# A two-layer feed-forward stage by seven products: when the next pair's first weights and its input are prepared

## The chip, the cores and the metric

The kernel runs on one core of one Trainium2 chip. The metric is the device time of one execution in microseconds (us); the median of three executions stands for a kernel. A "span" is the time from the first to the last instruction that the profiler recorded. PE is the matmul engine (PEld its weight loads), DVE the vector engine, ACT the scalar engine, POOL is GpSimd and SP the engine whose queue issues all DMAs here.

## The reference

Three things are computed one after the other: windowed attention, a gated feed-forward layer, and the layer that matters here, which takes its input `x` of 2304 tokens by 512:

```python
def _moe2_ref(x, w_in, w_out) -> np.ndarray:      # x 2304 x 512, w_in 512 x 2048, w_out 2048 x 512
    h = x @ w_in
    sp = np.where(h > 20.0, h, np.log1p(np.exp(np.minimum(h, 20.0))))
    g = h * np.tanh(sp)
    return (g @ w_out).astype(np.float32)
```

## The kernel before

The last layer is `layer2` (L739), some 380 us at the end of the span. It works on three **pairs** of token groups (`NPB` = 3, each of 2 x 384 tokens). Both of its products are done by a 2 x 2 scheme with seven products in place of eight (`ORDER1` and `ORDER2`, L742 and L743), whose operands are sums and differences of quarters of the matrices. Every float32 operand is split in two parts, a rounded one and the rest: `hi_act` (L123) writes the first on ACT, `lo_dve` (L126) the second on DVE, and `part` (L661) issues both. Three matmuls of 128 x 128 by 384 columns (`products`, L706) make one float32 product of the parts.

For each pair there are two stages, called the hidden and the out stage below.

**Hidden stage.** Eight blocks (`NJ` = 8, `hidden`, L769), each seven products of two chunks, so 42 matmuls a block and 336 a stage. Block j needs the weight tile `win[p, j]` with the seven combinations in two parts. `make_win` (L753) builds it: four subtractions on POOL into the single buffer `t4` (L758), then two `hi_act` and two `lo_dve` (the lines L124 and L127 of the profile). Its input is loaded by `load_raw` (L749, a DMA of 512 KB on SP into one of two buffers `w4`). In the loop (L827) block j first issues `make_win` for block j + 2 and `load_raw` for block j + 4, as long as these lie in the same pair. The sums that leave a block are added on DVE (`add`, L665 and its line L666) and go through an activation on ACT (`mish`, L1001) into the tiles `G`.

**Out stage.** The loop over `ORDER2` = 4, 1, 6, 7, 2, 5, 3 (L844): seven products, each over four operand tiles `op` (`operands`, L797), 28 tiles in all, 12 matmuls each. An operand tile is one `part` of a quarter of `G` (one ACT and one DVE instruction), and around it stand sums of quarters on DVE (L803 to L811). There are five `op` buffers, so tile n can be written only after PE has done with tile n - 5. The weights `wout` come by DMA, 1 MB for every two operand tiles, into three buffers. When a product is complete, `outputs` (L715) adds its bank on DVE into the tiles `u` (shown as `v` in this stage) and `y`.

**What is prepared for the next pair.** After the last block, `load_x` (L678) loads the next input into `xr` with two DMAs of 768 KB, and the first two `load_raw` of the next pair are issued (L835 to L838). After product 7 the seven input operands `xs` are made by `x_parts` (L690): seven `part` and four sums of quarters (`sums4`, L668), so 7 instructions on ACT and 11 on DVE. After products 2 and 5 the first two weight tiles of the next pair are built (L887 to L890). `xr` and the `win` tiles share the tag `win`, of which the pool `br` (L983) has three buffers; a buffer is taken up again when its last reader is done.

**What sets the order.** PE's order is the order of the program (`manual_schedule`, L892). The queues of ACT, DVE, POOL and SP are put in order when the program is built (`schedule_with_timeline_sim`, L1052): by a modelled timeline, within what the data and the buffers allow, so that work may stand on its queue long before the place where the program names it. On the chip each queue then runs in that fixed order. `tc.issue_after(ins)` puts what is traced under it, on the engine of `ins`, behind `ins` on that engine's queue; it adds no wait for `ins` to finish.

Of the kernel before, what the change touches and what calls it, by code (L numbers as in the profile page):

```python
# [9 lines left out]
F32 = mybir.dt.float32  # L10
# [4 lines left out]
AF = mybir.ActivationFunctionType  # L15
ALU = mybir.AluOpType
# [11 lines left out]
NPB = NT // (2 * TB)  # L28
NJ = NF2 // 2
# [67 lines left out]
def body(ctx: ExitStack, tc: tile.TileContext, qT, kT, vP, w1, w1o, w2, cst, yT):  # L97
    nc = tc.nc
# [22 lines left out]


    def hi_act(out, in_):  # L123
        nc.scalar.activation(out=out, in_=in_, func=AF.Copy)  # L124

    def lo_dve(out, in_, hi):  # L126
        nc.vector.tensor_tensor(out=out, in0=in_, in1=hi.bitcast(F32), op=ALU.subtract)  # L127

    plansA = []
    t = 0  # L130
# [523 lines left out]
    def bank():  # L654
# [3 lines left out]
            return rot("bk")  # L658
        return ps.tile([128, 512], F32, tag=f"acc{c % CT}", name="bk", bufs=1)

    def part(x, src):  # L661
        hi_act(x[:, 0], src)
        lo_dve(x[:, 1], src, x[:, 0])

    def add(out, a, b, op=ALU.add):  # L665
        nc.vector.tensor_tensor(out=out, in0=a, in1=b, op=op)  # L666
# [20 lines left out]
    def x_tiles(bp, which):  # L687
        return {i: bp.tile([128, 2, 2, TB], F32R, tag=f"xs{i}", name=f"xs{i}", bufs=1) for i in which}
# [50 lines left out]
    def layer2(br):  # L739
        G = {}  # L740
        win, wout = {}, {}
        ORDER1 = (1, 6, 7, 5, 2, 4, 3)  # L742
        ORDER2 = (4, 1, 6, 7, 2, 5, 3)  # L743
        onto = {2: 1, 3: 5}
        onto2 = {2: 1}

        raws = {}

        def load_raw(p, j):  # L749
            raws[p, j] = br.tile([128, 4, 256], F32, tag="w4", name="w4", bufs=2)  # L750
            nc.sync.dma_start(out=raws[p, j], in_=w2d[j].rearrange("p (k n) -> p k n", k=4))

        def make_win(p, j):  # L753

            w = raws.pop((p, j))
            x = t4
            for o, a, b in ((0, w[:, 0], w[:, 1]), (1, w[:, 3], x[:, 0]), (2, w[:, 3], w[:, 0]), (3, x[:, 1], w[:, 2])):
                nc.gpsimd.tensor_tensor(out=x[:, o], in0=a, in1=b, op=ALU.subtract)  # L758
            t = win[p, j] = br.tile([128, 2, 7, 256], F32R, tag="win", name="win")
            for d, src in ((slice(0, 3), w[:, 1:4]), (slice(3, 7), x)):  # L760
                hi_act(t[:, 0, d], src)
                lo_dve(t[:, 1, d], src, t[:, 0, d])

        def load_wout(p, i, k):
            t = bp.tile([128, NJ // 2, 2, 256], F32R, tag="wout", name="wout", bufs=3)
            wout[p, i, k] = t
            nc.sync.dma_start(out=t.bitcast(F32), in_=w2o[SLOT[i], :, k * (NJ // 2):(k + 1) * (NJ // 2)])

        def hidden(p, j, xs):  # L769
            w = win.pop((p, j))  # L770
            q, jj = divmod(j, 2)
            if jj == 0:
                G[p, q] = bp.tile([128, 4, 2, TB], F32, tag=f"g{q}", name="G", bufs=1)
            g = G[p, q]
            u = {}

            def new():
                return bp.tile([128, TB], F32, tag="u", name="u", bufs=6)

            def done(k, a, b):  # L780
                if b is None:
                    mish(g[:, k, jj], a)
                    return
                add(g[:, k, jj], a, b, ALU.subtract if k == 2 else ALU.add)
                mish(g[:, k, jj], g[:, k, jj])

            bks = {}
            for i in ORDER1:
                bk = bks[i] = bks[onto[i]] if i in onto else bank()
                s = SLOT[i]  # L790
                products(
                    bk, [(w[:, 0, s, c:c + 128], w[:, 1, s, c:c + 128]) for c in (0, 128)],
                    [(xs[i][:, 0, c], xs[i][:, 1, c]) for c in range(2)], i not in onto, i not in onto.values(),
                )
                outputs(i, bk, u, new, done, True)

        def operands(p, i):  # L797

            for q in range(NJ // 2):
                g = G[p, q]  # L800
                o = bp.tile([128, 2, 2, TB], F32R, tag="op", name="op", bufs=5)
                if i == 6:
                    add(g[:, 0], g[:, 3], g[:, 0], ALU.subtract)  # L803
                part(o, g[:, {4: 3, 1: 0, 6: 0, 7: 2, 2: 1, 5: 3, 3: 2}[i]])
                yield o
                if i == 4:
                    add(g[:, 3], g[:, 2], g[:, 3])
                if i == 1:
                    add(g[:, 2], g[:, 0], g[:, 2], ALU.subtract)
                if i == 7:  # L810
                    add(g[:, 2], g[:, 1], g[:, 0], ALU.subtract)  # L811

        load_raw(0, 0)
        t4 = br.tile([128, 4, 256], F32, tag="t4", name="t4", bufs=1)
        xs = x_tiles(br, (7, 5))
        xr = load_x(br, 0)
        xs.update(x_tiles(br, (1, 4, 6, 2, 3)))
        load_raw(0, 1)
        x_parts(xs, xr)
        for j in range(2):  # L820
            make_win(0, j)
            load_raw(0, j + 2)
        bp, mish = yield
        yr = yT.rearrange("(c p) t -> p c t", p=128)
        for p in range(NPB):
            loads = [(i, k) for i in ORDER2 for k in range(2)]
            for j in range(NJ):  # L827
                if j + 2 < NJ:
                    make_win(p, j + 2)
                if j + 4 < NJ:  # L830
                    load_raw(p, j + 4)
                if j >= NJ - 3:
                    load_wout(p, *loads.pop(0))
                hidden(p, j, xs)
            if p + 1 < NPB:  # L835
                xr = load_x(br, p + 1)
                for j in range(2):
                    load_raw(p + 1, j)  # L838
            us = [{}, {}]
            ys = [[bp.tile([128, 2, TB], F32, tag="y", name="y", bufs=4) for _ in range(2)] for _ in range(2)]  # L840
            held = {}
            left = [[2, 2], [2, 2]]
            t0 = 2 * p * TB
            for i in ORDER2:  # L844
                bks = held[i] = held[onto2[i]] if i in onto2 else [bank(), bank()]
                for q, o in enumerate(operands(p, i)):
                    k, jq = divmod(2 * q, NJ // 2)
                    if (p, i, k) not in wout:
                        load_wout(p, i, k)
                        loads.remove((i, k))  # L850
                    w = wout[p, i, k]
                    if jq == 0 and loads:
                        load_wout(p, *loads.pop(0))
                    for m in range(2):
                        products(
                            bks[m],
                            [(w[:, jq + e, 0, 128 * m:128 * m + 128], w[:, jq + e, 1, 128 * m:128 * m + 128]) for e in range(2)],
                            [(o[:, 0, e], o[:, 1, e]) for e in range(2)],
                            i not in onto2 and q == 0, i not in onto2.values() and q == NJ // 2 - 1,
                        )  # L860
                for m in range(2):

                    def done(k, a, b, m=m):
                        t, f = divmod(k, 2)
                        y = ys[f][m]
                        if b is None:
                            nc.scalar.activation(out=y[:, t], in_=a, func=AF.Copy)
                        else:
                            add(y[:, t], a, b, ALU.subtract if k == 2 else ALU.add)
                        left[f][m] -= 1  # L870
                        if not left[f][m]:
                            nc.sync.dma_start(out=yr[:, 2 * f + m, t0:t0 + 2 * TB], in_=y.rearrange("p a t -> p (a t)"))

                    def new():
                        return bp.tile([128, TB], F32, tag="u", name="v", bufs=6)

                    if i == 4:
                        us[m]["p4"] = bks[m][:, :TB]
                        continue
                    outputs(i, bks[m], us[m], new, done, False)  # L880
                    if i == 7:
                        done(2, us[m]["b"], us[m]["p4"])
                if p + 1 < NPB:
                    if i == 7:
                        xs = x_tiles(br, range(1, 8))
                        x_parts(xs, xr)
                    if i in (2, 5):  # L887
                        j = (2, 5).index(i)
                        make_win(p + 1, j)
                        load_raw(p + 1, j + 2)  # L890

    with tc.manual_schedule(engines={mybir.EngineType.PE}):  # L892
        nc.sync.dma_start(out=cst_sb, in_=cst)
# [25 lines left out]
        while at < lasts[0]:  # L919
# [11 lines left out]
            f = (at / lasts[0] - CFG["conv_a"]) / (CFG["conv_b"] - CFG["conv_a"])  # L931
# [124 lines left out]
```

## Time and profile before

| | us |
|---|---|
| median of three executions | 1024.19 |
| lowest and highest of the three | 1022.73 and 1025.08 |
| the profiled execution | 1022.81 |
| its span | 1021.0 |
| layer 2 in it, first to last matmul | 637.0 to 1017.2 |

The profiled execution took 1.8 us more than its span: that lies around the recorded instructions. In the timeline view a row is a start, a length, an engine, a source line and an operation with its output and input; several like instructions in a row are merged ("x3"), and a bracket gives the idle time of the engine ahead of it and what ended that. In the view by windows each engine has its busy time and its instructions in the stretch, then come the granted clock of PE as a share of full speed, the DMA share and GB/s. The mean length of an instruction on DVE or ACT holds some overlap with the next one: of two in a row the starts are what counts.

### The profile page before, as it was taken

To read this page: it belongs to the slowest core of one execution; us is meant where nothing else is said; L and a number is where in the kernel's file an instruction comes from. 1 tells how busy PE (TensorE), PEld (TensorE's weight loads), DVE (VectorE), ACT (ScalarE), POOL (GpSimd) and SP (SyncE) were. 2 spreads that over 40 slices of the span, in tenths; PEclk is the share of its full clock that TensorE was granted. 3 is DMA by queue.
4 is the path that set the end of the run, shared out by engine and by line. 5 is a ranking of instruction groups with operands and counts; after the bars stand their busy time and mean duration, and the time that the engine had idled before them with its cause. 6 is when DMAs were issued, how large, how long until landed. Compare 5 with 4: busy or idle time off the path is not lost.

```text
span 1021.0 us, 14513 instructions
## 1 busy us (share of the span) xinstructions
PE 982.3 (96%) x5168; PEld 861.5 (84%) x5168; DVE 704.1 (69%) x1247; ACT 550.5 (54%) x1121; POOL 183.2 (18%) x204
## 2 busy tenths in 40 slices
PE   7899999999999999999999999599999999999998
PEld 5566777899987777787888999599899998999998
DVE  5988887777667644558643666877974888757773
ACT  6867565767666654545543345456453564335442
POOL 3700000000000000000002342542821429113000
PEclk9989999999999999999999999799999999999999
DMA  8844423476354622336401997513685236850275
GB/s 314 287 193 134 158 80 115 146 245 204 84 186 142 225 84 61 110 111 235 159 22 63 329 367 257 210 63 104 226 288 187 83 121 231 292 160 21 69 258 189
DMA packets 74936, 173.90 MB, mean 170 GB/s; under 512 B 8432, under 2 KB 50032, under 8 KB 65136
## 3 DMA queue, kind: packets, MB, share of 16 engines
q1 hardware_dynamic: 74864, 172.98, 51.0%
q8 instruction: 40, 0.66, 0.2%
q14 instruction: 32, 0.26, 0.1%
HBM read 137.30 MB, written 35.65 MB: 169 GB/s over the span
## 4 chain that ended last, share of the span: by engine, by line
PE 77%; DVE 8%; DMA 5%; POOL 5%; ACT 2%; issue 2%; SPq 1%; DVEq 0%; ACTq 0%; POOLq 0%
PE g_ps L117 28%; PE bk L117 24%; PE acc L117 14%; PE o_ps L117 5%; POOL t L758 4%; PE s_ps L117 4%; PE t_ps L259 3%; DMA wout<-w2o 2%; DVE G L666 1%; DVE win L127 1%; DMA wraw<-w 1%; DVE op L127 1%; POOL Pt L249 1%; DVE xs L127 1%; DVE xr L666 1%
## 5 line engine op out<-in xcount | busy, mean ns | idle before, releaser
L117 PE MATMUL g_ps<-xt,w 128*128 128x512 f32 (+1 forms) x1440 | 322.2, 375 | 0.3 <-ACT PT L271 0.3
L117 PEld LDWEIGHTS g_ps<-xt,w 128*128 128x128 f32 x1440 | 259.5, 188 | 40.3 <-issue 3.3
L117 PE MATMUL bk<-xs,win 128*128 128x384 f32 x1008 | 179.4, 337 | 14.2 <-ACT xs L124 8.0
L117 PEld LDWEIGHTS bk<-xs,win 128*128 128x128 f32 x1008 | 176.4, 189 | 16.9 <-ACT xs L124 8.3
L117 PE MATMUL bk<-op,wout 128*128 128x384 f32 x1008 | 180.9, 340 | 6.4 <-DVE op L127 4.9
L117 PEld LDWEIGHTS bk<-op,wout 128*128 128x128 f32 x1008 | 177.6, 191 | 9.2 <-DVE op L127 6.7
L117 PE MATMUL acc<-hh,ring 128*128 128x512 f32 (+1 forms) x480 | 149.7, 374 | 0.0
L758 POOL TENSOR_TENSOR t<-w 128x256 f32<-128x256 f32 x48 | 82.3, 1735 | 195.6 <-DVE win L127 184.5
L117 PEld LDWEIGHTS acc<-hh,ring 128*128 128x128 f32 x480 | 89.0, 188 | 13.8 <-issue 1.9
L124 ACT ACTIVATE op<-G 128x768 fp32r<-128x768 f32 x84 | 69.1, 841 | 47.3 <-PE bk L117 44.1
L127 DVE TENSOR_TENSOR op<-G,op 128x768 fp32r<-128x768 f32 x84 | 79.5, 957 | 21.7 <-ACT op L124 21.6
L117 PE MATMUL acc<-hl,ring 128*128 128x512 f32 (+1 forms) x240 | 88.4, 368 | 0.0
L230 ACT ACTIVATE Pt<-Pt,sm 128x256 f32<-128x256 f32 (+2 forms) x160 | 74.6, 467 | 16.7 <-DVE sm L226 16.3
L226 DVE CUSTOM_DVE_ANT_0 Pt<-s_ps,cst_sb 128x256 f32<-128x256 f32 (+2 forms) x160 | 54.3, 376 | 34.9 <-PE s_ps L117 34.8
L602 ACT ACTIVATE t<-g_ps 128x512 f32<-128x512 f32 (+1 forms) x60 | 33.1, 551 | 78.3 <-PE g_ps L117 78.3
L603 DVE SCALAR_TENSOR_TENSOR t<-t,g_ps 128x512 f32<-128x512 f32 (+1 forms) x60 | 37.7, 628 | 52.5 <-ACT t L602 52.4
L611 DVE SCALAR_TENSOR_TENSOR t<-t,g_ps 128x512 f32<-128x512 f32 (+1 forms) x60 | 37.9, 632 | 43.6 <-PE g_ps L117 42.7
L209 POOL MEMSET sm<- 128x8 f32 x40 | 5.3, 144 | 338.4 <-ACT Pt L247 310.2
L541 POOL TENSOR_TENSOR cw<-cw 128x256 f32<-128x256 f32 x32 | 30.4, 971 | 192.7 <-DMA cw<-w2d 192.2
L666 DVE TENSOR_TENSOR G<-u,bk 128x384 f32<-128x384 f32 x72 | 39.3, 553 | 36.0 <-PE bk L117 33.8
L1001 ACT ACTIVATE G<-G 128x384 f32<-128x384 f32 x72 | 37.0, 519 | 49.3 <-DVE G L666 49.3
L124 ACT ACTIVATE hh<-t 128x512 fp32r<-128x512 f32 (+1 forms) x60 | 34.9, 582 | 52.6 <-DVE t L611 52.6
(71 smaller groups left out, 1313.3 us busy)
## 6 DMA issues: line engine op xcount, KB each, us to landing
wout<-w2o SPq DMA_DIRECT2D x42, 1024.0 KB, 5.4
wraw<-w SPq DMA_DIRECT2D x16, 1024.0 KB, 5.4
w2o<-chl SPq DMA_DIRECT2D x16, 896.0 KB, 5.9
wst<-w SPq DMA_DIRECT2D x12, 1024.0 KB, 8.0
cw<-w1od SPq DMA_DIRECT2D x24, 512.0 KB, 4.0
w<-w2d SPq DMA_DIRECT2D x24, 512.0 KB, 3.4
w2d<-cw SPq DMA_DIRECT2D x16, 512.0 KB, 3.6
wraw<-w1o SPq DMA_DIRECT2D x6, 1024.0 KB, 6.0
```

Of the source, the lines that this page charges most:

```text
L117: nc.tensor.matmul(out=out, lhsT=lhsT, rhs=rhs, start=start, stop=stop, skip_group_check=True)
L124: nc.scalar.activation(out=out, in_=in_, func=AF.Copy)
L127: nc.vector.tensor_tensor(out=out, in0=in_, in1=hi.bitcast(F32), op=ALU.subtract)
L226: nc.vector.tensor_tensor_reduce(out=Pt[:q.qn, :w], in0=s_ps[:q.qn, q.so:q.so + w], in1=nb[:q.qn, 128 - q.kn:128 + q.qn], op0=ALU.add, op1 ...
L230: nc.scalar.activation(out=Pt[:q.qn, :w], in_=Pt[:q.qn, :w], func=AF.Exp, scale=-1.0, bias=sm[:q.qn, i:i + 1], accum_out=sm[:q.qn, 8 + i:9 ...
L259: nc.tensor.transpose(t_ps[:x.n, o:o + q.qn], Pt[:q.qn, c0:c0 + x.n], ident[:q.qn, :q.qn])
L602: tanhs.append(nc.scalar.activation(out=t[:, :n], in_=st["g"][:, :n], func=AF.Tanh, scale=0.5))
L603: nc.vector.scalar_tensor_tensor(out=t[:, :n], in0=t[:, :n], scalar=1.0, in1=st["g"][:, :n], op0=ALU.add, op1=ALU.mult)
L611: nc.vector.scalar_tensor_tensor(out=t[:, :n], in0=t[:, :n], scalar=0.5, in1=vps[:, :n], op0=ALU.mult, op1=ALU.mult)
L666: nc.vector.tensor_tensor(out=out, in0=a, in1=b, op=op)
L758: nc.gpsimd.tensor_tensor(out=x[:, o], in0=a, in1=b, op=ALU.subtract)
L1001: nc.scalar.activation(out=out, in_=in_, func=AF.Mish)
```

## The change

`make_win` and `load_raw` run on over the end of a pair: the blocks j = 6 and 7 build the first two weight tiles of the next pair, the blocks 4 to 7 load the raw weights of its first four. The calls after the last block and after products 2 and 5 go. `part` keeps the two instructions that it issued last, and `x_parts` is called under `tc.issue_after` for both: its ACT instructions stand behind the last ACT instruction of product 7's operands, its DVE instructions behind the last such DVE instruction.

```diff
     def hi_act(out, in_):
-        nc.scalar.activation(out=out, in_=in_, func=AF.Copy)
+        return nc.scalar.activation(out=out, in_=in_, func=AF.Copy)
 
     def lo_dve(out, in_, hi):
-        nc.vector.tensor_tensor(out=out, in0=in_, in1=hi.bitcast(F32), op=ALU.subtract)
+        return nc.vector.tensor_tensor(out=out, in0=in_, in1=hi.bitcast(F32), op=ALU.subtract)
...
+    latest = []
+
     def part(x, src):
-        hi_act(x[:, 0], src)
-        lo_dve(x[:, 1], src, x[:, 0])
+        latest[:] = hi_act(x[:, 0], src), lo_dve(x[:, 1], src, x[:, 0])
...
             for j in range(NJ):
-                if j + 2 < NJ:
-                    make_win(p, j + 2)
-                if j + 4 < NJ:
-                    load_raw(p, j + 4)
+                for f, k in ((make_win, p * NJ + j + 2), (load_raw, p * NJ + j + 4)):
+                    if k < NPB * NJ:
+                        f(*divmod(k, NJ))
                 if j >= NJ - 3:
                     load_wout(p, *loads.pop(0))
                 hidden(p, j, xs)
             if p + 1 < NPB:
                 xr = load_x(br, p + 1)
-                for j in range(2):
-                    load_raw(p + 1, j)
...
-                if p + 1 < NPB:
-                    if i == 7:
-                        xs = x_tiles(br, range(1, 8))
+                if p + 1 < NPB and i == 7:
+                    xs = x_tiles(br, range(1, 8))
+                    with tc.issue_after(latest[0].ins), tc.issue_after(latest[1].ins):
                         x_parts(xs, xr)
-                    if i in (2, 5):
-                        j = (2, 5).index(i)
-                        make_win(p + 1, j)
-                        load_raw(p + 1, j + 2)
+
```

## Rows read from the trace of the kernel before

**Rows 1.** The page, part 1: busy time, share of the span, instructions
```profile
PE 982.3 (96%) x5168; PEld 861.5 (84%) x5168; DVE 704.1 (69%) x1247; ACT 550.5 (54%) x1121; POOL 183.2 (18%) x204
```
**Rows 2.** Windows: the out stages of the three pairs, one after the other
```profile
711.02:774.28 63.26, 60.82 (x338) 59.69 (x337) 50.19 (x61) 29.50 (x40) 27.30 (x8) 0.97 0.71 243
...
833.85:898.35 64.50, 61.07 (x337) 59.63 (x337) 50.18 (x61) 29.50 (x40) 27.29 (x8) 0.97 0.70 238
...
957.94:1017.75 59.81, 58.71 (x337) 58.09 (x336) 38.11 (x48) 22.28 (x30) 0.00 (x0) 1.00 0.64 208
```
**Rows 3.** Timeline of PE, from the first pair's hidden stage to the end
```profile
672.95 14.86 PE L117 MATMUL bk<-xs,win 128*128 128x384 f32 x84 [0.52 <-DVE G L666]
688.02 23.16 PE L117 MATMUL bk<-xs,win 128*128 128x384 f32 x132 [0.21 <-DVE G L666]
...
732.37 14.47 PE L117 MATMUL bk<-op,wout 128*128 128x384 f32 x72 [1.99 <-DVE op L127]
747.30 27.14 PE L117 MATMUL bk<-op,wout 128*128 128x384 f32 x155 [0.46 <-DVE op L127]
...
855.20 14.45 PE L117 MATMUL bk<-op,wout 128*128 128x384 f32 x72 [1.98 <-DVE op L127]
...
889.95 8.56 PE L117 MATMUL bk<-op,wout 128*128 128x384 f32 x48 [0.98 <-DMA wout<-w2o]
...
957.94 50.11 PE L117 MATMUL bk<-op,wout 128*128 128x384 f32 x288
1008.57 8.59 PE L117 MATMUL bk<-op,wout 128*128 128x384 f32 x48 [0.51 <-DMA wout<-w2o]
```
**Rows 4.** Windows within the first pair's out stage, and within the third's
```profile
711.02:730.39 19.37, 19.37 (x110) 18.70 (x109) 19.37 (x23) 12.89 (x19) 11.03 (x1) 1.00 0.62 204
...
732.37:740.00 7.63, 7.63 (x35) 7.63 (x36) 6.03 (x7) 1.46 (x2) 7.63 (x3) 0.78 0.43 140
...
977.30:991.35 14.05, 14.05 (x83) 14.05 (x82) 11.08 (x14) 5.59 (x7) 0.00 (x0) 1.00 0.80 268
991.35:1017.75 26.40, 25.30 (x145) 24.68 (x143) 12.26 (x18) 7.66 (x10) 0.00 (x0) 1.00 0.59 197
```
**Rows 5.** Timeline of all engines around the start of the first out stage
```profile
703.93 0.85 ACT L124 ACTIVATE win<-w 128x768 fp32r<-128x768 f32 x1
...
719.36 20.32 POOL L758 TENSOR_TENSOR t<-w 128x256 f32<-128x256 f32 x2 [8.63 <-DVE win L127]
...
720.07 0.95 DVE L127 TENSOR_TENSOR op<-G,op 128x768 fp32r<-128x768 f32 x1
...
721.81 0.95 DVE L127 TENSOR_TENSOR xs<-xr,xs 128x768 fp32r<-128x768 f32 x1
...
725.28 0.95 DVE L127 TENSOR_TENSOR xs<-xr,xs 128x768 fp32r<-128x768 f32 x1
726.15 0.95 DVE L666 TENSOR_TENSOR G<-G 128x768 f32<-128x768 f32 x1
...
727.35 0.84 ACT L124 ACTIVATE op<-G 128x768 fp32r<-128x768 f32 x1
...
741.23 1.06 ACT L124 ACTIVATE win<-t 128x1024 fp32r<-128x1024 f32 x1 [6.29 <-POOL t L758]
```
**Rows 6.** The weight tile's POOL line L758 by tile: lengths min/median/max in ns
```profile
L758 POOL TENSOR_TENSOR t<-t,w x24: 728/741/1338, 629.8 to 935.2; 128x256 f32<-128x256 f32 x24
```
**Rows 7.** Timeline of DVE in the third out stage, around product 7's last operand
```profile
981.93 0.96 DVE L127 TENSOR_TENSOR op<-G,op 128x768 fp32r<-128x768 f32 x1
...
984.60 0.95 DVE L127 TENSOR_TENSOR op<-G,op 128x768 fp32r<-128x768 f32 x1
...
991.12 1.01 DVE L666 TENSOR_TENSOR v<-v,bk 128x384 f32<-128x384 f32 x2
```
**Rows 8.** Timeline of SP: the first pair's loads of the next input and of `wout`
```profile
696.65 1.20 SPq L682 DMA_DIRECT2D xr<-x2d  x2
...
715.39 0.33 SPq L767 DMA_DIRECT2D wout<-w2o  x1
```

## The prediction

> **What bounds the kernel.** The page's first part comes first: PE is busy for 96% of the span and DVE for 69% [rows 1], so a gain must come from time that PE loses, and only a stage in which DVE is short can lose it. The windows by stage show where that is. The three out stages do the same 336 matmuls, yet the first two take 63.26 and 64.50 us from their first matmul to the next stage's, and in both DVE is busy for 50.2 us; the third prepares no next pair, DVE has 38.1 us of work, and it takes 59.22 us (957.94 to 1008.57 + 8.59) [rows 2, 3]. The reader is to see that the two stages that prepare the next pair lose 4.04 and 5.28 us against the third, 9.32 us together. That is the whole stake at the pair boundaries.
>
> The timeline of PE says what the loss is made of. In the first pair PE waits 1.99 us for an operand's DVE part. In the next 7.63 us the granted clock is 0.78, so part of the time is at the lower of PE's two levels, 1.2 in place of 2.4 GHz, and the 72 matmuls take 14.47 us. At the third stage's rate (50.11 us for 288, 0.174 us each) they would take 12.53, so the clock costs 1.94 us more. A wait of 0.46 us follows [rows 3, 4]. The second pair repeats it, with 1.98 us, and adds a wait of 0.98 us for `wout`; the third has such a `wout` wait too, 0.51 us [rows 3].
>
> Why the operand is late is read from the windows inside the stage: from 711.02 to 730.39 DVE is busy for 19.37 of 19.37 us, while in the third stage it has gaps [rows 4]. The timeline of the engines names what fills it: between the operand parts stand input operands `xs`, as at 721.81 and 725.28, and weight parts. POOL shows it from the other side: two subtractions take 20.32 us [rows 5], where one takes 0.74 [rows 6]. An ACT instruction of a weight tile then stands at the head of ACT's queue for 6.29 us waiting for POOL [rows 5], with operand parts behind it.
>
> **The order on the queues.** The timeline also shows how the builder orders work. The sum at 726.15 is for product 6's second operand, whose first part is made at 727.35. Its last input was free after the operand of 720.07, yet input work that the program names much later (721.81, 725.28) went ahead of it [rows 5]. So what is ready first is queued first, wherever the program names it. Two things follow: before, input and weight work was drawn into the crowded first third of the stage because it was ready; after, input work tied behind product 7 need not hold back product 2's operands until all of it is done.
>
> **The change part by part.** *Input work leaves the first two thirds of the out stage.* It is 7 ACT and 11 DVE instructions. A DVE one takes 0.95 us, and in a row 0.87 from start to start (725.28 to 726.15 [rows 5]), so 9.6 us of DVE. Two weight-part instructions (about 2.1 us at the same spacing) go too, and the next tile's POOL work falls earlier. The stage up to product 7 is then like the third's, in which PE did not wait for an operand. I take the third's 59.22 us for both: a gain of 9.32 us. It keeps a `wout` wait of 0.51 us in each; bounds 0 and 0.98 [rows 3].
>
> *It goes behind product 7.* In the third stage the last operand part of product 7 is issued at 981.93 and product 2's first at 984.60. PE reaches that operand after 16 tiles of 12 matmuls, at 957.94 + 16 x 2.09 = 991.4. So the operand ends 5.8 us before it is needed [rows 3, 7]. DVE has 3.0 us free from 977.30 to 991.35 and 14.1 us after that [rows 4], 17.1 for 9.6. At most three or four input parts are ready at once, since most wait for a sum and each sum for the one before: an operand that queues behind what was ready earlier waits for 4 x 0.87 = 3.5 us, and at the end of product 7 also for its four adds, 1.9 us (1.01 for two that overlap, [rows 7]). Together 5.4 us, under the 5.8: cost 0. The margin is thin, so the other end, no mixing at all, is the first rival. On ACT seven parts stand behind product 7's last; ACT is busy for 5.59 of 14.05 us there [rows 4], so they are covered; without that cover each would delay an operand by its 0.84 us [rows 5].
>
> *The weight tiles move into blocks 6 and 7.* Each is four POOL subtractions, two ACT and two DVE instructions and a load. Before, the first was already in block 7 (ACT at 703.93) and the second at the start of the out stage [rows 5]; now each is a block or so earlier, as in blocks 0 to 5. Blocks 3 and 5 begin with waits of 0.52 and 0.21 us for DVE, since the blocks ahead of them hold an operand, its sums and a weight tile together [rows 3]. Block 6 has the same mix, so block 7 will begin with such a wait; bounds 0 and 0.52. I take 0.3, nearer to block 5's, whose neighbour it resembles: 0.6 us for two pairs.
>
> *The input's load comes later.* It takes the buffer of the third tile back, and the two weight tiles now stand ahead of it: not block 5's, free at the time of its issue at 696.65, but block 7's, free at about 711 [rows 8]. Its two DMAs stand on SP ahead of the `wout` load of 715.39 and take 1.20 us to issue, so they delay nothing. The data is wanted only at product 7, more than 20 us later: cost 0; at worst the 1.5 MB slow that `wout` load by as much as the worst `wout` wait seen, 0.98 us [rows 3]. The four raw loads move into the hidden stage; those that SP issued between `wout` loads no longer can hold them up. The third weight tile takes the input's buffer after the input work, late in the stage: 2.1 us of DVE that fit into what is left of the 17.1; block 2 needs it only in the next stage.
>
> Sum: -9.32 + 0.6 = -8.7 us. Against the profiled execution, 1022.81, that is 1014.1; the median of the three runs is 1.4 us higher, so I forecast a median of 1015.5.
>
> **A rule weighed.** The two subtractions of 20.32 us ran beside a DVE with no gap, and alone such a one takes 0.74 [rows 5, 6]: the two engines exclude each other. The Trainium skill ("SBUF — State Buffer", section "SBUF: two separate sides") says that DVE and GpSimd share one port pair, and that whichever starts first holds it for the whole instruction. The trace agrees for POOL. The rule also speaks against the change, as the third rival works out: POOL's work is put beside DVE in blocks 6 and 7.
>
> **The rivals.**
> *Input work in one go* (slower). If all 11 DVE instructions are queued ahead of product 2's first operand, that begins not at 984.60 but 9.6 us later, at 994.2. By then product 7 is done and its adds (1.9 us) come first; the operand ends at 997.0, and PE, ready at 991.4, waits 5.6 us. The clock then costs 1.94 us, as after the wait of 1.99. Two pairs: +15.1 on the sum, so 1029.2 for the profiled execution and 1030.6 for the median. It decides if fewer than about two of product 2's four operands get in between. For it: the program names the input work first. Against: the order seen at 726.15. Chance 0.11.
> *Half mixed.* The operands come late by some 2 us, because the input work and product 7's adds meet. That is the very stall of before, 1.99 + 1.94, moved by five tiles: +7.9 on the sum, a median of 1023.4. For it: the margin of 0.4 us. Chance 0.14.
> *POOL holds DVE in blocks 6 and 7.* Four subtractions a tile hold it up to 4 x 0.74 = 3.0 us, and two tiles a pair, if none of it is hidden, 6.0 us, with the clock's 1.94: two pairs +15.9, a median of 1031. Against: blocks 2 and 4 have the same subtractions, and PE lost 0.52 and 0.21 us there. Chance 0.03.
> *Nothing moves.* Other work that is ready fills the same stretch (the third weight tile), DVE stays full and the time is that of before, 1024. Against: that tile has no buffer until the input work is done. Chance 0.02.
>
> **The numbers.** The forecast has 0.70. A measurement of this kernel can tell about 0.2%, 2 us, from no change. The half-mixed case lies at the edge of that: I count 0.03 of it faster, 0.09 same, 0.02 slower. With the other rivals: faster 0.73, same 0.12, slower 0.15. The range begins at 1012.5: all the time that the two stages spend above 336 x 0.174 = 58.5 us is 10.8, from the median 1013.4, with 0.9 us for the spread of the runs. It ends at 1023.5, with the half-mixed case in it; what is left out is 0.16.
>
> **What would show it.** Right: both out stages near 59 to 60 us, no PE wait over 1 us at an operand, the granted clock 1.00 throughout, no POOL subtraction of many us, `xr` issued at about 711, input parts between product 2's operands, block 7 beginning with 0.2 to 0.5 us of wait. Wrong: a wait of 2 to 6 us at the operands of product 2 with a lower clock behind it (first and second rival), or PE waits for DVE in blocks 6 and 7 (third).

## The result and the profile after

The changed kernel takes a median of 1013.45 us (1012.0 to 1015.74, four runs) against 1024.63 us for the kernel before in the same runs: a ratio of 0.990, with a 95% interval of 0.9883 to 0.9916. It is faster, by 11.2 us where 8.7 were forecast. The profiled execution took 1012.0 us, 10.8 less than that of before. In the rows below the lines from L666 up to the loop are shifted by one (`add` is L667, the POOL subtractions are at L759).

The windows of the three out stages after the change (columns as in [rows 2]):

```profile
710.82:769.08 58.26, 58.26 (x337) 58.26 (x337) 48.38 (x60) 28.95 (x39) 2.86 (x4) 1.00 0.81 279
...
829.17:887.44 58.27, 58.27 (x338) 58.27 (x338) 48.38 (x60) 28.93 (x39) 2.87 (x4) 1.00 0.80 275
...
947.01:1006.36 59.35, 58.70 (x337) 58.09 (x336) 37.55 (x47) 22.27 (x30) 0.00 (x0) 1.00 0.61 208
```

They answer to [rows 2]. The first two went from 63.26 and 64.50 to 58.26 and 58.27 us, 11.2 us together, the whole gain; in both PE is busy throughout and the granted clock is 1.00. DVE still has 48.4 us of work there, against 50.2 before: the work did not go, it was spread. In the first third of the stage, where DVE was busy for 19.37 of 19.37 us [rows 4], it is now busy for 14.79 of 19.38:

```profile
710.82:730.20 19.38, 19.38 (x113) 19.38 (x113) 14.79 (x18) 9.19 (x14) 0.00 (x0) 1.00 0.78 260
```

The timeline of PE shows both stages without a gap:

```profile
672.25 14.85 PE L117 MATMUL bk<-xs,win 128*128 128x384 f32 x84 [0.52 <-DVE G L667]
687.30 14.86 PE L117 MATMUL bk<-xs,win 128*128 128x384 f32 x84 [0.20 <-DVE G L667]
702.37 8.60 PE L117 MATMUL bk<-xs,win 128*128 128x384 f32 x48 [0.22 <-DVE G L667]
710.82 58.43 PE L117 MATMUL bk<-op,wout 128*128 128x384 f32 x336
769.08 20.99 PE L117 MATMUL bk<-xs,win 128*128 128x384 f32 x120
...
829.17 58.43 PE L117 MATMUL bk<-op,wout 128*128 128x384 f32 x336
...
997.77 8.59 PE L117 MATMUL bk<-op,wout 128*128 128x384 f32 x48 [0.65 <-DMA wout<-w2o]
```

The operand waits of 1.99, 0.46 and 1.98 us and the `wout` wait of 0.98 us of [rows 3] are gone from the first two stages. What is new is the wait at 702.37, shown as 0.22 us. It comes after 288 matmuls of the hidden stage, six blocks of 42 and 36 of block 6 (the blocks are counted from 0), so ahead of block 6's last product, six matmuls before block 7. That product is summed onto the bank (the buffer of a product's sum) of product 5, which DVE's `add` into `G` reads first. The stretch from the wait before it to the stage's end takes 23.52 us (687.30 to 710.82) where before it was 23.00 (688.02 to 711.02 [rows 2, 3]): the new wait costs 0.52.

DVE and ACT around product 7's last operand, in the timeline of both:

```profile
733.92 0.85 ACT L124 ACTIVATE op<-G 128x768 fp32r<-128x768 f32 x1 [1.23 <-PE bk L117]
734.67 2.30 ACT L124 ACTIVATE xs<-xr 128x768 fp32r<-128x768 f32 x3
...
734.80 0.96 DVE L127 TENSOR_TENSOR op<-G,op 128x768 fp32r<-128x768 f32 x1
...
738.34 1.82 DVE L127 TENSOR_TENSOR xs<-xr,xs 128x768 fp32r<-128x768 f32 x2
740.08 1.82 DVE L127 TENSOR_TENSOR op<-G,op 128x768 fp32r<-128x768 f32 x2
741.82 0.95 DVE L667 TENSOR_TENSOR xr<-xr 128x768 f32<-128x768 f32 x1
742.69 1.82 DVE L127 TENSOR_TENSOR op<-G,op 128x768 fp32r<-128x768 f32 x2
```

Three input parts stand at once behind product 7's operand; then operands of product 2 and input work alternate. The first of product 2's operands ends at 741.03 (740.08 + 0.95), and PE needs it at 710.82 + 16 x 2.09 = 744.2.

POOL and SP, in their timelines:

```profile
699.75 2.08 POOL L759 TENSOR_TENSOR t<-w 128x256 f32<-128x256 f32 x2 [5.01 <-DVE win L127]
706.87 1.43 POOL L759 TENSOR_TENSOR t<-w 128x256 f32<-128x256 f32 x2 [3.53 <-DVE win L127]
764.72 1.43 POOL L759 TENSOR_TENSOR t<-w 128x256 f32<-128x256 f32 x2 [54.90 <-DVE win L127]
```
```profile
711.01 1.20 SPq L683 DMA_DIRECT2D xr<-x2d  x2
715.19 37.76 SPq L768 DMA_DIRECT2D wout<-w2o  x10
```

No pair of subtractions is near the 20.32 us of [rows 5]: the third tile's run at 706.87, in block 7. The input is loaded at 711.01 in place of 696.65 [rows 8].

### The profile page after: what moved, and what is told of

It is laid out like the page before. It is cut to its first block, busy times and chain, and to the rows that moved or that the text cites. A ratio compares the mean times of both kernels' runs of the same rounds, so it can differ in the third digit from the quotient of the medians.

```text
span 1010.2 us, 14509 instructions
## 1 busy us (share of the span) xinstructions
PE 977.5 (97%) x5168; PEld 859.2 (85%) x5168; DVE 702.8 (70%) x1247; ACT 552.0 (55%) x1121; POOL 140.7 (14%) x204
## 4 chain that ended last, share of the span: by engine, by line
PE 84%; DVE 6%; DMA 4%; ACT 3%; issue 1%; POOL 1%; SPq 1%; DVEq 0%; ACTq 0%; POOLq 0%
PE bk L117 31%; PE g_ps L117 28%; PE acc L117 14%; PE o_ps L117 5%; PE s_ps L117 3%; PE t_ps L259 3%; DVE G L667 1%; ACT Pt L230 1%; DMA w2d<-cw 1%; DMA wout<-w2o 1%; POOL Pt L249 1%; DMA wraw<-w1o 1%; DVE win L127 1%; DMA cw<-w1od 1%; DVE u L667 1%
## 5 line engine op out<-in xcount | busy, mean ns | idle before, releaser
L117 PE MATMUL bk<-xs,win 128*128 128x384 f32 x1008 | 180.4, 338 | 14.6 <-ACT xs L124 8.0
L117 PE MATMUL bk<-op,wout 128*128 128x384 f32 x1008 | 175.6, 334 | 0.7 <-DMA wout<-w2o 0.7
L117 PEld LDWEIGHTS bk<-op,wout 128*128 128x128 f32 x1008 | 174.8, 188 | 0.9 <-issue 0.9
L230 ACT ACTIVATE Pt<-Pt,sm 128x256 f32<-128x256 f32 (+2 forms) x160 | 74.6, 468 | 16.4 <-DVE sm L226 15.9
L759 POOL TENSOR_TENSOR t<-w 128x256 f32<-128x256 f32 x48 | 41.6, 888 | 229.0 <-DVE win L127 218.0
L667 DVE TENSOR_TENSOR G<-u,bk 128x384 f32<-128x384 f32 x72 | 39.1, 552 | 35.8 <-PE bk L117 33.6
L247 ACT ACTIVATE Pt<-Pt,sm 128x256 f32<-128x256 f32 (+2 forms) x128 | 50.2, 464 | 7.2 <-DVE sm L241 6.8
```

Source lines behind the costliest of these rows:

```text
L117: nc.tensor.matmul(out=out, lhsT=lhsT, rhs=rhs, start=start, stop=stop, skip_group_check=True)
L230: nc.scalar.activation(out=Pt[:q.qn, :w], in_=Pt[:q.qn, :w], func=AF.Exp, scale=-1.0, bias=sm[:q.qn, i:i + 1], accum_out=sm[:q.qn, 8 + i:9 ...
L247: nc.scalar.activation(out=pt, in_=pt, func=AF.Copy, scale=r)
```

## The experiments

Theory: before, DVE had more to do ahead of the early operands than time, and the clock and POOL's hold on ACT made the loss larger; anything that takes enough DVE work out of the first third repairs it, provided that the moved work mixes with the operands. The first rival: both parts of the change are needed. The second: the place after product 7 is free by itself, mixed or not. The weight tiles alone, the tie alone, the input work in one go and the tie behind the last product ran side by side with the kernel before (1024.47 us), and so did the other four (1025.19 us).

### The weight tiles alone

Against the changed kernel:

```diff
-                    with tc.issue_after(latest[0].ins), tc.issue_after(latest[1].ins):
-                        x_parts(xs, xr)
+                    x_parts(xs, xr)
```

> The weight tiles move as in the change, but the input work is not tied. My theory: PE lost time only because DVE had more in the first third of the out stage than fits ahead of the operands. With the weight tiles gone and the input loaded only at about 711, the input work starts at about 718; up to product 6's second operand DVE has 16 instructions of 0.87 us, ends near 726, and PE needs it at 729.6: no wait over 1 us, out stages 58.3 to 59.3, time within 2 us of the changed kernel (1012 to 1016). Rival (both parts are needed): an operand wait of about 2 us with the clock's 1.9 stays in both stages, 1020 to 1024.

Measured: 1015.74 us (1015.15 to 1015.9), ratio 0.9908 (0.9877 to 0.9939). The first two out stages in the timeline of PE:

```profile
711.95 50.46 PE L117 MATMUL bk<-op,wout 128*128 128x384 f32 x288
762.97 8.77 PE L117 MATMUL bk<-op,wout 128*128 128x384 f32 x48 [0.55 <-DMA wout<-w2o]
...
831.64 50.30 PE L117 MATMUL bk<-op,wout 128*128 128x384 f32 x288
882.34 8.76 PE L117 MATMUL bk<-op,wout 128*128 128x384 f32 x48 [0.39 <-DMA wout<-w2o]
```

No operand wait is left; only waits for `wout` are. The stages take 59.62 us (711.95 to 771.57) and 59.29. So not both parts are needed. The input work starts on DVE at 717.90 (before: 707.37), after its load at 712.15: with three buffers, the weight tiles cannot come earlier without the input's load coming later, so this kernel delays the input work too, by some 10 us, without a tie.

### The tie alone

```diff
                         xs = x_tiles(br, range(1, 8))
-                        x_parts(xs, xr)
+                        with tc.issue_after(latest[0].ins), tc.issue_after(latest[1].ins):
+                            x_parts(xs, xr)
```

It stands on the kernel before, with `latest` and the returned instructions as in the change.

> The input work is tied behind product 7, the weight tiles stay where they were. My theory: only two weight-part instructions (2.1 us) remain in the first third, which the operands' lead covers; no operand wait over 1 us, and block 7 begins without the 0.5 us that the changed kernel pays there, so 1012 to 1014, level with the changed kernel or up to 1 us under it. Rival (both parts are needed, because POOL's subtractions for the third tile starve again beside a full DVE and hold ACT): POOL subtractions of over 10 us, ACT waits of several us, 1018 to 1024.

Measured: 1014.69 us (1013.38 to 1016.41), ratio 0.9901 (0.9872 to 0.9929). PE and POOL in their timelines:

```profile
712.38 58.43 PE L117 MATMUL bk<-op,wout 128*128 128x384 f32 x336
770.65 20.99 PE L117 MATMUL bk<-xs,win 128*128 128x384 f32 x120
...
830.22 58.43 PE L117 MATMUL bk<-op,wout 128*128 128x384 f32 x336
```
```profile
718.43 9.90 POOL L759 TENSOR_TENSOR t<-w 128x256 f32<-128x256 f32 x2 [7.05 <-DVE win L127]
```

The tie alone makes the out stages as short as the whole change does. POOL's two subtractions are still held for 9.90 us, but nobody waits: the third tile's parts follow only after the input work. So a long POOL instruction is no loss by itself.

To tell the two apart the tie alone and the change were run again, five rounds each.

> The tie alone, timed again beside the changed kernel. My theory: the move of the weight tiles brings nothing beside the tie and costs 0.5 us a pair at block 7, so 0 to 1.5 us under the changed kernel, hardly to be told apart in time (1012 to 1015); in the profile layer 2 is 1 us shorter. Rival: the move brings something that one profile did not show, and the tie alone is 1 us or more slower.

> The changed kernel again, for the comparison with the tie alone and with the version whose start is ordered: 1012 to 1015, out stages 58.3 us, 0.5 us lost at block 7 in the first two pairs.

Measured: 1013.9 us for the tie alone (ratio 0.9898, 0.988 to 0.9917) and 1014.69 us for the change (0.990, 0.9884 to 0.9917). Time can't separate them. In the profiles layer 2, from its second product to its last matmul, takes 355.53 us with the tie alone (652.33 to 1007.86) and 356.81 with the change (652.55 to 1009.36). Of this difference of 1.28 us, 1.0 is the 0.5 us ahead of block 7 in two pairs, which only the change has. So in these profiles the move of the weight tiles added nothing to the tie and cost about 1 us.

### The input work in one go

Against the changed kernel; the loop over a product's operands stands between the two added parts:

```diff
+                held_back = ExitStack()
+                if i == 2 and p + 1 < NPB:
+                    for x in latest:
+                        held_back.enter_context(tc.issue_after(x.ins))
                 for q, o in enumerate(operands(p, i)):
...
+                held_back.close()
```

> The changed kernel with product 2's operands tied behind the last input part, so the 11 DVE instructions run ahead of them in one go: the prediction's first rival, forced. My theory (mixing is what makes the place after product 7 free): product 2's first operand ends near 749.9 where PE needs it at 744.3, a wait of 5.6 us, and the clock falls behind it for 1.9 us: 7.5 us a pair, 1028.5 (1025 to 1031). Rival (product 7's place alone is what matters, five operands of lead cover the block): waits under 2 us, 1013 to 1018.

Measured: 1030.64 us (1029.77 to 1035.24), ratio 1.0069 (1.0044 to 1.0094): slower than the kernel before. PE in the first of the two stages:

```profile
712.83 33.50 PE L117 MATMUL bk<-op,wout 128*128 128x384 f32 x192
750.16 0.69 PE L117 MATMUL bk<-op,wout 128*128 128x384 f32 x1 [3.83 <-ACT op L124]
752.09 18.59 PE L117 MATMUL bk<-op,wout 128*128 128x384 f32 x95 [1.23 <-DVE op L127]
```

Sixteen operands run (192 matmuls), then PE waits from about 746.3 to 752.1, with one matmul in between, where 5.6 us were worked out; the next 95 matmuls take 18.59 us where 0.174 us each would give 16.5, 2.1 us for the clock (granted 0.74 from 752.09 to 760.00). The stages take 66.98 and 66.21 us. The place behind product 7 is free only because the queue mixes.

### The tie behind the last product

Against the changed kernel:

```diff
-                if p + 1 < NPB and i == 7:
+                if p + 1 < NPB and i == 3:
```

> The changed kernel with the input work tied behind the last product, 3, in place of 7. My theory: the out stages stay at 58.3 us, but the operand for the next stage's second product (6) is finished near 771.6, about 1.5 us after PE wants it, since two of the input instructions stand behind the last adds: each next hidden stage starts with a wait of 1 to 2 us and perhaps the clock's 1.9: 1015 to 1020. Rival (any place after the first third is as good): 1012 to 1015.

Measured: 1019.56 us (1018.77 to 1019.92), ratio 0.9948 (0.9931 to 0.9964). The start of the next hidden stages in the timeline of PE:

```profile
772.77 1.40 PE L117 MATMUL bk<-xs,win 128*128 128x384 f32 x7
775.61 19.91 PE L117 MATMUL bk<-xs,win 128*128 128x384 f32 x113 [1.43 <-DVE xs L127]
...
892.87 1.40 PE L117 MATMUL bk<-xs,win 128*128 128x384 f32 x7
896.18 19.86 PE L117 MATMUL bk<-xs,win 128*128 128x384 f32 x113 [1.90 <-DVE xs L127]
```

The out stages stay short (58.99 and 58.27 us), and PE waits 1.43 and 1.90 us at the next stage's second product, as worked out. So the place has a late bound: not so late that the next stage is hungry. An early bound is not shown, since with the weight tiles moved the untied input work cost no operand wait in the first two thirds.

### Two weight instructions fewer in the first third

This is the kernel before with the input work left where it was; only the second weight tile's ACT and DVE instructions are tied behind product 7 (`tail` is `latest` as it was there).

```diff
-                        make_win(p + 1, j)
+                        with ExitStack() as es:
+                            for x in tail if j else ():
+                                es.enter_context(tc.issue_after(x.ins))
+                            make_win(p + 1, j)
```

> The kernel before with one edit: the ACT and DVE instructions of the second weight tile (2.1 us of DVE) are tied behind product 7; the input work stays where it was and starts before the out stage does. My theory (the wait before was a matter of amount: DVE had some 2 us more to do ahead of product 6's second operand than time): with two instructions fewer, and the third tile's behind them, that operand ends near 728.5 where PE needs it at 729.8, so no wait over 0.5 us, no fall of the clock, 1013 to 1017. Rival (the early input work alone makes the wait): about 2 us of operand wait and the clock's 1.9 stay in both pairs, 1020 to 1024.

Measured: 1019.66 us (1018.72 to 1023.41), ratio 0.9948 (0.9934 to 0.9963): between the two expectations. The timelines say why:

```profile
713.56 42.83 PE L117 MATMUL bk<-op,wout 128*128 128x384 f32 x246
757.41 7.56 PE L117 MATMUL bk<-op,wout 128*128 128x384 f32 x42 [1.02 <-DVE y L667]
766.47 8.59 PE L117 MATMUL bk<-op,wout 128*128 128x384 f32 x48 [1.49 <-DMA wout<-w2o]
```
```profile
744.55 6.43 POOL L759 TENSOR_TENSOR t<-w 128x256 f32<-128x256 f32 x2 [31.27 <-DVE win L127]
...
753.24 1.06 ACT L124 ACTIVATE win<-t 128x1024 fp32r<-128x1024 f32 x1 [5.33 <-POOL t L759]
754.21 2.30 ACT L124 ACTIVATE op<-G 128x768 fp32r<-128x768 f32 x3
754.34 1.23 DVE L127 TENSOR_TENSOR win<-t,win 128x1024 fp32r<-128x1024 f32 x1 [2.54 <-ACT win L124]
756.35 1.01 DVE L667 TENSOR_TENSOR y<-v,bk 128x384 f32<-128x384 f32 x2
756.41 0.85 ACT L868 ACTIVATE y<-bk 128x384 f32<-128x384 f32 x2
```

The early wait is gone, with 2.1 us of DVE work taken away and the input work as early as before: 246 matmuls run without a gap, twenty operands and half of the next. So that wait was a matter of amount, not of early input work as such. But 5.33 us of ACT's queue are lost later, behind a weight part that waits for POOL. DVE's part of the same tile then waits 2.54 us for ACT, and what stands behind the two comes late: operand parts, and on DVE the adds into `y`, for which PE waits 1.02 us. The `wout` waits, 1.49 and 1.26 us, cost as much again. The stages take 61.33 and 61.08 us. My expectation left out that the POOL hold moves with the tile, and it had no term for `wout`. The hold is a second mechanism of the kernel before (6.29 us on ACT [rows 5]); the wait of PE that followed there was 0.46 us.

### The same means at the start of layer 2

The timeline of PE at the first pair shows it waiting for input operands there too, in all the kernels above: 7.96 us for an ACT part and 4.03 us for a DVE part. On top of the tie alone, the last chunk's copies (`evacuate`) were tied behind the first two input parts (`first_x` holds the second's two instructions; the expectation says three), and the second tile's parts behind all of the first input work.

```diff
-        for j in range(2):
-            make_win(0, j)
-            load_raw(0, j + 2)
+        make_win(0, 0)
+        load_raw(0, 2)
+        with tc.issue_after(latest[0].ins), tc.issue_after(latest[1].ins):
+            make_win(0, 1)
+        load_raw(0, 3)
...
+                    for x in first_x[:2] if ci == len(plansA) - 1 else ():
+                        es.enter_context(tc.issue_after(x.ins))
                     evacuate(acc, p.n, x2d[:, :, p.t0:p.t0 + p.n])
```

> The tie alone, and the same means at the start of layer 2: the last chunk's copies out of PSUM stand behind the first three input parts on ACT and DVE, and the second weight tile's parts behind all of the first pair's input work. My theory (queues ordered by when things were thought ready hold up the first operands there too): product 6's operand is whole near 646 instead of 652.4, the second wait of 4 us goes, 5 to 6.5 us less than the tie alone: 1007 to 1010. Rival (POOL's subtractions beside the sums, or block 1's weight tile coming late, take it back): within 2 us of the tie alone.

Measured: 1010.08 us (1008.77 to 1011.5), ratio 0.9851 (0.9829 to 0.9873); the interval lies below that of the change in the same runs. PE in the timeline, of the tie alone and of this kernel:

```profile
647.62 0.69 PE L117 MATMUL bk<-xs,win 128*128 128x384 f32 x1 [7.96 <-ACT xs L124]
652.33 21.25 PE L117 MATMUL bk<-xs,win 128*128 128x384 f32 x113 [4.03 <-DVE xs L127]
```
```profile
645.46 0.44 PE L117 MATMUL bk<-xs,win 128*128 128x384 f32 x1 [4.47 <-ACT xs L124]
647.19 15.15 PE L117 MATMUL bk<-xs,win 128*128 128x384 f32 x71 [1.29 <-DVE xs L127]
662.85 7.58 PE L117 MATMUL bk<-xs,win 128*128 128x384 f32 x42 [0.51 <-DVE G L670]
671.52 14.86 PE L117 MATMUL bk<-xs,win 128*128 128x384 f32 x84 [1.10 <-DVE G L670]
```

The two waits fall from 12.0 to 5.8 us. From layer 2's first matmul to the end of the second wait, 6.5 us are won (7.43 us, 639.76 to 647.19, where the tie alone takes 13.89, 638.44 to 652.33). Up to the last product of block 2, 2.6 us of it are lost again (24.33 us where the tie alone takes 21.76): the granted clock is 0.64 from 647.19 to 655.00, where behind the second wait of the tie alone it is 0.80 (652.33 to 660.00), a wait of 0.51 us is new, and one of 1.10 is longer than the 0.51 it was. That the later start of the weight tiles makes these two longer is likely, but not shown. The gain over the tie alone is 3.8 us where I expected 5 to 6.5. It is the fastest kernel of this study.

## Why the prediction was right

**The stake.** It was put at the two out stages that prepare a next pair, and they gave 11.2 us. The kind was right; the size was short by the measure chosen. I took the third stage's 59.22 us, which holds a `wout` wait, and bounded that wait by 0; it was 0 in both stages, which took 58.27, so 0.96 us more each. The step that was mis-sized is "I take the third's 59.22 us for both". In all four profiles of the change and of the tie alone the `wout` wait was 0 in both stages; why was not settled, so that this bound held is not explained. The floor under the range, 58.5 us a stage, was set too high by the same measure: PE without a gap took 58.27.

**Input work out of the first two thirds.** Right, and more than needed: the tie alone gives all of it. The prediction put the gain down to both parts together; the runs show that either is enough to end the operand waits, since 2.1 us of DVE less already removes the early one.

**Behind product 7.** Cost 0, as taken. The queue mixed, as read from the order at 726.15 [rows 5], and the smallest lead of the operands looked at was 3.2 us where a bound of 0.4 was left. The forced rival gives its price: 5.8 us of wait, one matmul in it, and 2.1 for the clock, where 5.6 and 1.94 were worked out. That rival is therefore a real one; what decided against it was the order.

**Weight tiles in blocks 6 and 7.** I took 0.3 us a pair between bounds of 0 and 0.52; it was the upper bound, 0.52. The mechanism came as read, and the bracket shows 0.22 us, like the 0.21 that the 0.3 leant on. What was mis-sized is that the bracket was taken for the cost: the 84 matmuls up to the wait and the wait itself take 15.07 us (687.30 to 702.37), where 0.174 us each makes 14.6. The waits also lie six matmuls ahead of blocks 3, 5 and 7, and not at their starts. POOL holding DVE there, the third rival, did not come: the subtractions at 706.87 took 1.43 us for two.

**The input's load later.** Cost 0, as taken; `xr` was issued at 711.01.

**The account.** Of the 10.8 us between the profiled executions, the first two out stages give 11.2, the wait ahead of block 7 takes back 1.0. The rest lies outside the change: layer 2's first matmul came 1.1 us earlier, its first blocks took 0.4 us more and the third out stage 0.1. In the chances the rivals add up to 0.11 for the same and 0.16 for slower, not 0.12 and 0.15.

## What to carry to other kernels

A queue in fixed order that was filled by what is ready first takes in work that nobody needs yet, just where the engine is short: look in the trace for work that is due much later among instructions that PE waits for, and tie it behind the last of these. Tie it where what follows can mix with it; the same work in one block took 1030.64 us here, against 1013.45. Of two edits that relieve the same engine in the same stretch, run each alone before their gains are added.

## What had not been expected of the hardware

Two POOL subtractions took 20.32 us beside a DVE without gaps [rows 5], 9.90 with the tie alone and 6.43 in the run with the late tile, against 1.43 at 706.87 after the change: POOL was held not for one DVE instruction but for a whole run of them. At 706.87 DVE was not idle either:

```profile
706.71 1.20 DVE L667 TENSOR_TENSOR u<-u,bk 128x384 f32<-128x384 f32 x2
```

These adds take one input from a bank of PE's products, and POOL's two subtractions beside them took no longer than the 0.74 us each of [rows 6]. The instructions that stood beside the long subtractions have both inputs in tiles, and are longer (128x768 or 128x1024); with the late tile the two subtractions got through beside the first pair of bank adds (DVE at 749.61, POOL's end at 750.98). So a busy DVE alone does not hold POOL; whether the place of the inputs or the length decides was not separated by a run.

PE's waits of about 1 us (0.98 [rows 3], 1.02 and 1.10 above) cost no more than themselves, with a granted clock of 1.00 behind each. The waits of 1.99 and 1.98 us were followed by 0.78 and 0.77 (732.37 to 740.00, 855.20 to 862.50 before) and cost some 1.9 us more. The long waits at the start of layer 2 cost 1.6 to 3.0 us more: 113 matmuls in 21.25 to 22.65 us in the runs that left that start as it was, where 0.174 each makes 19.66. But the wait of 1.90 us with the tie behind the last product was followed by 1.00 (896.18 to 903.00). What sorts these cases was not settled, and no run was made for it. Nor was it settled why the `wout` waits (0 to 1.49 us) come in some stages and not in others.
